# Loads of batch 2's u rows bound behind batch 1's v rows, and two units' row swaps moved from VectorE to DMA

## The chip, the cores and the metric

The kernel runs on one core of a Trainium2 chip. The metric is device time in microseconds (us) of one execution. A core has a matrix engine (TensorE, PE in the profile, with its weight loads as PEld), VectorE (DVE), ScalarE (ACT), GpSimd (POOL) and SyncE (SP), each with an instruction stream of its own that runs in order; they meet at semaphores. SP and POOL issue DMAs, which run on 16 DMA engines.

## The reference

Two layers, one after the other. The first mixes in the frequency domain: a real FFT over the 3008 positions of each of 8 batches (256 channels), a complex 256x256 product with a bias, a soft threshold, and the inverse FFT. The second is a two-layer network over all 24064 rows.

```
def _attn_ref(x, w_r, w_i, b_r, b_i):
    X = np.fft.rfft(x, axis=1)
    Xr, Xi = (X.real.astype(np.float32), X.imag.astype(np.float32))
    Yr = Xr @ w_r - Xi @ w_i + b_r
    Yi = Xr @ w_i + Xi @ w_r + b_i
    lam = 0.01
    Yr = np.sign(Yr) * np.maximum(np.abs(Yr) - lam, 0.0)
    Yi = np.sign(Yi) * np.maximum(np.abs(Yi) - lam, 0.0)
    Y = Yr.astype(np.float64) + 1j * Yi.astype(np.float64)
    return np.fft.irfft(Y, n=x.shape[1], axis=1).astype(np.float32)

def _moe_ref(x, w_in, w_out, s, b):
    h = x @ w_in                      # 256 -> 2048
    r = np.maximum(h, 0.0)
    g = s * (r * r) + b
    return (g @ w_out).astype(np.float32)   # 2048 -> 256
```

## The kernel before

The FFTs are done as matrix products, in two factors each (3008 = 94 x 32 for batches 0 and 1, 64 x 47 for the others). One batch passes through these steps, all with fp16 operands and fp32 in PSUM:

- **u** (`s1_units`, matmul L701 for batch 1, L703 for the others): the first factor of the forward DFT. The copies out of PSUM (`evac`, L248 on ACT or L252 on DVE) go to tiles u, which SP stores to a DRAM buffer ud (L707).
- **us** (`load_us`, L716): four SP loads per batch bring the u rows back in another order, 384 KB each. For batch 1 they follow the last store at once; for the others they are units of the plan (`us_loads`).
- **forward, second factor**: L768 for batch 1 (`fwd_unit` inside `mix_units`), L734 for the others (`fwd_units`), into xt.
- **mix** (`mix_units`): for each of 12 units i, `sum_unit` (L798) and `mix_unit` (L811) do the complex product; DVE adds (L816, which frees the PSUM bank), clips (L821, L822) and subtracts (L823) in slots of a tile called ring. Then four **row swaps** per unit copy 64-row blocks of the result to another slot of ring (lines 827 to 834), either as SP DMAs of 32 KB (L831) or as DVE copies (L833).
- **inverse, first factor** (`inv_unit`, L841): reads the swapped slot four units later; every second unit SP stores v to a DRAM buffer vd (L850, six stores of 256 KB per batch). After the last unit SP loads the v rows back in two loads of 768 KB (L857, tiles vs).
- **inverse, second factor** (`s4_units`, L897): from vs into yt, the rows of the second layer.

The second layer (`first_mm` L952 with the Relu on ACT L959 and the square on ACT L963 or DVE L966; `second_mms` L1010 with the scaling on DVE L1020 and output stores L978, L985 and L993) runs over tiles of 512 (or 480) rows in 16 slots each, the second product one tile behind the first. After a first stage for batch 0 alone, this stream is the backbone: a plan written out by hand (`schedule`) places the units of the other batches' DFTs into its slots. Units of batch 1's `mix_units` lie in slots 24 to 65; batch 2's u loads in slots 75 to 82; `s4_units(1)` begins 11 slots, and `fwd_units(2)` 6 slots, before batch 1's rows begin in the second layer.

The order in which each engine's instructions stand is made by a scheduler when the program is built; `tc.issue_after(ins)` adds an edge, so that what is issued in the block stands behind `ins` on the same engine. Two further things set the order around the change. `evac` and `first_mm` choose between ACT and DVE by a running account of both engines' work (`load`), to which each swap on DVE adds 0.13. And SP's queue is in order: an SP DMA whose data aren't ready, or that must wait for an earlier DMA, holds all behind it.

Of the kernel before, what the change touches and what calls it, by code (L numbers as in the profile page):

```python
# [165 lines left out]
def kernel(  # L166
# [507 lines left out]

    UCH = XCH // 2
    us_loads = {}

    def s1_units(b, more_banks=False):

        old = b == 1  # L680
        rows, n = (96, N2) if old else (P, XH)
        ud = dpool.tile([rows, n, D], F16, name="ud", tag="ud")
        hold = {}
        if old:
            xts[b] = bigpool.tile([P, 2 * DC * CLASSES * L1], F16, name="xt", tag="xt")

        def unit(i):
            c, j = divmod(2 * i, XCH)
            k, ju = divmod(2 * i, UCH)
            if ju == 0:  # L690
                if old and k % 2:
                    w = UCH * D
                    hold["u"] = xts[b][:, k // 2 * w : k // 2 * w + w].rearrange(
                        "p (j d) -> p j d", d=D
                    )
                else:
                    hold["u"] = upool.tile([P, UCH, D], F16, name="u", tag="u")
            ps = any_bank() if more_banks else one_bank()
            rhs = x16[(b, c)][:, j * D : (j + 2) * D]
            if old:  # L700
                nc.tensor.matmul(ps[0:96, :], A_t[0:N1, :], rhs[0:N1], start=True, stop=True)  # L701
            else:
                nc.tensor.matmul(ps, A_2, rhs, start=True, stop=True)  # L703
            u = hold["u"]
            evac(u[0:rows, ju : ju + 2, :], ps[0:rows].rearrange("p (j d) -> p j d", j=2), 512)
            if ju == UCH - 2:
                nc.sync.dma_start(out=ud[:, k * UCH : (k + 1) * UCH, :], in_=u[0:rows])  # L707
            if i == n // 2 - 1 and old:
                for q in range(4):
                    load_us(q)  # L710

        def load_us(q):
            p, g = (P, 6) if old else (2 * SLOTS, GROUPS // 4)
            uv = ud.rearrange("k n d -> (k n) d").rearrange("(q p) d -> p q d", p=p)
            t = uspool.tile([P, g, D], F16, name="us", tag="us")
            nc.sync.dma_start(out=t[0:p], in_=uv[:, g * q : g * q + g, :])  # L716
            us[(b, q)] = t

        us_loads[b] = [lambda q=q: load_us(q) for q in range(4)]
        return [lambda i=i: unit(i) for i in range(n // 2)]  # L720

# [24 lines left out]
    def mix_units(b):  # L746

        old = b == 1
        vd = dpool.tile([NPAIR, P, D], F16, name="vd", tag="vd")
        if not ring:  # L750
            ring.append(bigpool.tile([P, 12, 2, D], F16, name="ring", tag="corr"))
        zt = {}
        hold = {}

        def xf(i):
            w = 3 * DC * P
            i %= 4
            return xts[b][:, w * i : w * i + w].rearrange("p (r c k) -> p r c k", r=3, c=DC)

        def fwd_unit(i):  # L760

            bank = one_bank()
            ps = bank.rearrange("p (r c j k) -> p r c j k", r=2, c=DC, j=2)
            t = us[(b, i // 3)]
            for j in range(2):
                q = (2 * i + j) % 6
                for dc in range(DC):
                    nc.tensor.matmul(  # L768
                        ps[:, :, dc, j, :], t[:, q, dc * P : (dc + 1) * P],
                        F_t[:, 2 * i + j, :], start=True, stop=True,  # L770
                    )
            xt = xf(i)
            evac(xt[:, 1:3].rearrange("p r c k -> p (r c k)"), bank, 512)
            nc.vector.tensor_tensor(out=xt[:, 0], in0=xt[:, 1], in1=xt[:, 2], op=ALU.add)
            load["dve"] += 0.25

        def xs_of(h):
            if old:
                return [xf(2 * h + i)[:, 0] for i in range(2)]
            xt = xts[b]  # L780
            at = slice(2 * P * h, 2 * P * h + 2 * P)
            xs = xspool.tile([P, DC, 2 * P], F16, name="xs", tag="xs")
            nc.vector.tensor_tensor(out=xs, in0=xt[:, 0, :, at], in1=xt[:, 1, :, at], op=ALU.add)
            load["dve"] += 0.38
            return [xs[:, :, i * P : (i + 1) * P] for i in range(2)]

        def x_of(i, r):
            if old:
                return xf(i)[:, 1 + r]
            return xts[b][:, r, :, i * P : (i + 1) * P]  # L790

        def sum_unit(h):

            xs = xs_of(h)
            ps = one_bank().rearrange("p (i e) -> p i e", i=2)
            for i in range(2):
                for dc in range(DC):
                    nc.tensor.matmul(  # L798
                        ps[:, i, :], xs[i][:, dc], W_g[:, dc, 2],
                        start=(dc == 0), stop=(dc == DC - 1),  # L800
                    )
            s = mpool.tile([P, 2, D], F32, name="s", tag="m")
            nc.scalar.copy(out=s, in_=ps)
            load["act"] += 0.6
            hold[h] = s

        def mix_unit(i):
            ps = one_bank().rearrange("p (r e) -> p r e", r=2)
            for r in range(2):
                for dc in range(DC):  # L810
                    nc.tensor.matmul(  # L811
                        ps[:, r, :], x_of(i, 1 - r)[:, dc], W_g[:, dc, r],
                        start=(dc == 0), stop=(dc == DC - 1),
                    )
            t, m = ring[0][:, i % 4], ring[0][:, 4 + i % 2]
            nc.vector.tensor_tensor(  # L816
                out=t, in0=ps, in1=hold[i // 2][:, i % 2].unsqueeze(1).to_broadcast([P, 2, D]),
                op=ALU.add,
            )

            nc.vector.tensor_tensor(out=m, in0=t, in1=low, op=ALU.max)  # L821
            nc.vector.tensor_tensor(out=m, in0=m, in1=high, op=ALU.min)  # L822
            nc.vector.tensor_tensor(out=t, in0=t, in1=m, op=ALU.subtract)  # L823
            load["dve"] += 1.75

            z = ring[0][:, 6 + i % 6]
            for j in range(2):
                for r in range(2):
                    o, a = z[64 * r : 64 * r + 64, j], t[64 * j : 64 * j + 64, r]
                    if i < (H // 2 if old else H - 2):  # L830
                        nc.sync.dma_start(out=o, in_=a)  # L831
                    else:
                        nc.vector.tensor_copy(out=o, in_=a)  # L833
                        load["dve"] += 0.13
            zt[i] = z

        def inv_unit(i):
            ps = one_bank().rearrange("p (j e) -> p j e", j=2)
            z = zt.pop(i)
            for j in range(2):  # L840
                nc.tensor.matmul(  # L841
                    ps[:, j, :], T_t[:, 2 * i + j, :], z[:, j, :], start=True, stop=True
                )
            if i % 2 == 0:
                hold["v"] = vpool.tile([P, 4, D], F16, name="v", tag="v")
            v = hold["v"]
            h = 2 * (i % 2)
            evac(v[:, h : h + 2, :], ps, 512)
            if i % 2 == 1:
                nc.sync.dma_start(  # L850
                    out=vd[2 * i - 2 : 2 * i + 2].rearrange("q p e -> p q e"), in_=v
                )
            if i == H - 1:
                vv = vd.rearrange("q (k n) e -> (q k) n e", n=N2)
                for h in range(2):
                    t = vspool.tile([96, HW, D], F16, name="vs", tag="vs")
                    nc.sync.dma_start(out=t, in_=vv[:, h * HW : (h + 1) * HW, :])  # L857
                    vs[(b, h)] = t

        units = []  # L860

        def put(f, i, n):
            if 0 <= i < n:
                units.append(lambda: f(i))

        for h in range(H // 2 + 2 + old):
            k = h - old
            if not old:
                put(sum_unit, h, H // 2)
            for i in range(2):  # L870
                if old:
                    put(fwd_unit, 2 * h + i, H)
                put(mix_unit, 2 * k + i, H)
                put(inv_unit, 2 * k - 4 + i, H)
            if old:
                put(sum_unit, h, H // 2)
            if k == H // 2 - 1:
                units += [lambda: None] * 2
        return units
# [238 lines left out]
```

## Time and profile before

| what | value |
|---|---|
| median of 3 runs | 846.5 us (846.5 to 850.94) |
| the profiled execution | 849.39 us |
| its span, first to last instruction | 847.6 us |
| mean granted TensorE clock | 0.998 |
| PE busy | 832.4 us (98%) |
| DVE busy | 692.2 us (82%) |
| ACT busy | 647.3 us (76%) |
| DMA queue of SP (q1) | 80.08 MB, 32.9% of 16 engines' span |
| DMA queue of POOL (q0) | 16.00 MB, 11.2% |

"Busy" counts the engine's instructions without those of its sequencer (waits and DMA issues). A wait table names who waited, for whom, and how long in total, how often and at most. A window of the profile gives per engine the busy us and the number of instructions (x), then the granted clock, the DMA engines' share and GB/s. Times inside the execution count from the span's start.

### The profile page before, as it was taken

The numbers are of one execution on the slowest core, as the hardware profiler recorded it, in microseconds if no ns is written. First come the engines' busy times: TensorE is split into PE (matmuls) and PEld (weight loads), VectorE is DVE, ScalarE is ACT, GpSimd is POOL, SyncE is SP. The second block draws the span as 40 slices with busy tenths as digits, with TensorE's granted clock in tenths as the row PEclk, the third lists the DMA queues.
The fourth block names the chain that finished last, engine by engine and source line by source line (L and its number), as shares of the span: only waits on it lengthen the run. The fifth ranks groups of instructions, "written<-read, shape, count | busy, mean of one in ns | idle before, by whom it ended". The sixth has DMA issues, their size and how long they took to land.

```text
span 847.6 us, 17209 instructions
## 1 busy us (share of the span) xinstructions
PE 832.4 (98%) x6726; PEld 597.9 (71%) x6726; DVE 692.2 (82%) x1011; ACT 647.3 (76%) x853; POOL 58.5 (7%) x87
## 2 busy tenths in 40 slices
PE   8999998999999999999999999999999999999998
PEld 6857675767777767766776767766677776766766
DVE  5999995888788888898888888888888878776674
ACT  5988875777887788788887887788777877766663
POOL 4640100000001000000001000000000000000000
PEclk9999999999999999999999999999999999999999
DMA  8965775156543674165722656023640222401111
GB/s 199 184 164 132 200 172 162 37 124 157 154 111 75 157 197 121 59 145 147 188 62 59 166 145 168 32 77 112 162 137 26 61 89 89 113 32 39 38 44 51
DMA packets 109225, 97.18 MB, mean 115 GB/s; under 512 B 10956, under 2 KB 98000, under 8 KB 107800
## 3 DMA queue, kind: packets, MB, share of 16 engines
q1 hardware_dynamic: 102200, 80.08, 32.9%
q0 software_dynamic: 6944, 16.00, 11.2%
q8 instruction: 53, 0.87, 0.4%
q14 instruction: 28, 0.23, 0.1%
HBM read 55.34 MB, written 46.66 MB: 120 GB/s over the span
## 4 chain that ended last, share of the span: by engine, by line
PE 86%; DVE 5%; DMA 3%; ACT 3%; issue 2%; POOL 0%; DVEq 0%; ACTq 0%; SPq 0%; POOLq 0%
PE psa L1010 36%; PE psh L952 35%; PE psf L811 4%; PE psf L897 2%; PE psf L841 2%; PE psf L734 2%; PE psf L798 2%; PE psf L703 2%; ACT rt L959 1%; DVE ring L816 1%; DMA x<-in_x_dram 1%; DVE gt L966 1%; PE psm L528 1%; DMA vd<-v 1%; DMA vs<-vd 1%
## 5 line engine op out<-in xcount | busy, mean ns | idle before, releaser
L959 ACT ACTIVATE rt<-psh 128x1024 f32<-128x1024 f32 (+2 forms) x384 | 387.1, 1009 | 111.3 <-PE psh L952 111.0
L966 DVE TENSOR_TENSOR gt<-rt 128x1024 f16<-128x1024 f32 (+2 forms) x319 | 380.6, 1197 | 103.4 <-ACT rt L959 101.0
L1010 PE MATMUL psa<-w_out_t,gt 128*128 128x256 f16 (+1 forms) x3024 | 455.1, 273 | 0.0
L1010 PEld LDWEIGHTS <-gt 128*128 128x128 f16 (+1 forms) x3024 | 301.3, 101 | 187.2 <-issue 2.0
L952 PE MATMUL psh<-yt,w_in 128*128 128x512 f16 (+1 forms) x1344 | 397.9, 378 | 0.2 <-ACT rt L959 0.2
L952 PEld LDWEIGHTS <-w_in 128*128 128x128 f16 x1536 | 140.8, 98 | 26.2 <-issue 3.5
L1020 DVE SCALAR_TENSOR_TENSOR ost<-psa,s_bc,bias_bc 128x512 f32<-128x512 f32 (+2 forms) x97 | 71.0, 732 | 14.3 <-PE psa L1010 13.3
L963 ACT ACTIVATE gt<-rt 128x1024 f16<-128x1024 f32 (+2 forms) x65 | 68.1, 1048 | 1.7
L248 ACT CAST v<-psf 128x512 f16<-128x512 f32 x83 | 48.1, 580 | 18.4 <-PE psf L841 17.1
L816 DVE TENSOR_TENSOR ring<-psf,s 128x512 f16<-128x512 f32 x84 | 57.4, 683 | 3.9 <-PE psf L811 2.3
L248 ACT CAST yt<-psf 128x480 f16<-128x480 f32 (+2 forms) x72 | 44.1, 623 | 17.2 <-PE psf L897 16.6
L952 PE MATMUL psh<-tail,w_in 128*128 128x512 f16 (+1 forms) x192 | 52.1, 353 | 0.0
L248 ACT CAST u<-psf 128x512 f16<-128x512 f32 (+1 forms) x71 | 41.7, 587 | 11.9 <-PE psf L703 11.8
L811 PE MATMUL psf<-W_g,xt 128*128 128x256 f16 x336 | 50.4, 273 | 0.0
L248 ACT CAST xt<-psf 128x480 f16<-128x480 f32 (+3 forms) x71 | 42.5, 599 | 9.0 <-PE psf L734 8.0
L916 POOL COPY tail<-yt 128x896 f16<-128x896 f16 x6 | 10.0, 1666 | 420.2 <-ACT yt L248 327.1
L821 DVE TENSOR_TENSOR ring<-ring,low 128x512 f16<-128x512 f16 x84 | 35.5, 422 | 2.2
L822 DVE TENSOR_TENSOR ring<-ring,high 128x512 f16<-128x512 f16 x84 | 35.4, 422 | 2.2
L823 DVE TENSOR_TENSOR ring<-ring 128x512 f16<-128x512 f16 x84 | 35.4, 422 | 1.8
L811 PEld LDWEIGHTS <-xt 128*128 128x128 f16 x336 | 32.9, 98 | 3.9
L897 PEld LDWEIGHTS <-vs 96*128 96x128 f16 x448 | 30.2, 98 | 6.5 <-DMA vs<-vd 3.8
L302 POOL DMA_DIRECT2D x<-in_x_dram x36 | 18.7, 528 | 222.9 <-PE psf L703 222.9
(114 smaller groups left out, 541.4 us busy)
## 6 DMA issues: line engine op xcount, KB each, us to landing
out_dram<-ost SPq DMA_DIRECT2D x170, 128.0 KB
us<-ud SPq DMA_DIRECT2D x28, 384.0 KB
vd<-v SPq DMA_DIRECT2D x42, 256.0 KB
vs<-vd SPq DMA_DIRECT2D x14, 768.0 KB
x<-in_x_dram POOLq DMA_DIRECT2D x36, 256.0 KB, 5.1
ud<-u SPq DMA_DIRECT2D x36, 256.0 KB
ring<-ring SPq DMA_DIRECT2D x264, 32.0 KB
out_dram<-ost SPq DMA_DIRECT2D x16, 120.0 KB
```

The costliest lines, as they stand in the source:

```text
L248: return None, nc.scalar.copy(out=dst, in_=src)
L811: nc.tensor.matmul(ps[:, r, :], x_of(i, 1 - r)[:, dc], W_g[:, dc, r], start=(dc == 0), stop=(dc == DC - 1),)
L816: nc.vector.tensor_tensor(out=t, in0=ps, in1=hold[i // 2][:, i % 2].unsqueeze(1).to_broadcast([P, 2, D]), op=ALU.add,)
L821: nc.vector.tensor_tensor(out=m, in0=t, in1=low, op=ALU.max)
L822: nc.vector.tensor_tensor(out=m, in0=m, in1=high, op=ALU.min)
L897: nc.tensor.matmul(ps[:, j * 96 : (j + 1) * 96], vs[(b, h)][:, k, ec * P : (ec + 1) * P], C_t if b == 1 else C_2, start=True, stop=True,)
L952: nc.tensor.matmul(o, w_in_t[dc][:, mc * P : (mc + 1) * P], r, start=(dc == 0), stop=(dc == DC - 1),)
L959: nc.scalar.activation(out=rt[:, :, 0:w], in_=ps[:, :, 0:w], func=AF.Relu)
L963: nc.scalar.activation(out=gt[:, :, 0:w], in_=rt[:, :, 0:w], func=AF.Square)
L966: nc.vector.tensor_tensor(out=gt[:, :, 0:w], in0=rt[:, :, 0:w], in1=rt[:, :, 0:w], op=ALU.mult)
L1010: nc.tensor.matmul(ps[0:size, h, :], gts[(ti, mc // 2)][:, mc % 2, sub * size : (sub + 1) * size], w_out_t[:, mc, :], start=(mc == 0), sto ...
L1020: nc.vector.scalar_tensor_tensor(out=ost[0:size, 0:k], in0=ps[0:size, 0:k], scalar=s_bc[0:size], in1=bias_bc[0:size].unsqueeze(1).to_broad ...
```

## The change

Three edits that belong to two changes. The u loads of batch 2 (L716) are issued inside `issue_after` of the last of batch 1's two v loads (L857), so they stand behind both on SP; before, nothing ordered them but the scheduler. And of batch 1's twelve units, units 6 and 7 make their row swaps as SP DMAs, as units 0 to 5 do, so that DVE copies those of units 8 to 11 alone; the running account of DVE's load is smaller by 8 x 0.13 from there on.

```
     us_loads = {}
+    last_vs = [None]
...
             t = uspool.tile([P, g, D], F16, name="us", tag="us")
-            nc.sync.dma_start(out=t[0:p], in_=uv[:, g * q : g * q + g, :])
+            if b == 2:
+                with tc.issue_after(last_vs[0].ins):
+                    nc.sync.dma_start(out=t[0:p], in_=uv[:, g * q : g * q + g, :])
+            else:
+                nc.sync.dma_start(out=t[0:p], in_=uv[:, g * q : g * q + g, :])
...
                     o, a = z[64 * r : 64 * r + 64, j], t[64 * j : 64 * j + 64, r]
-                    if i < (H // 2 if old else H - 2):
+                    if i < (H - 4 if old else H - 2):
                         nc.sync.dma_start(out=o, in_=a)
                     else:
                         nc.vector.tensor_copy(out=o, in_=a)
...
                     t = vspool.tile([96, HW, D], F16, name="vs", tag="vs")
-                    nc.sync.dma_start(out=t, in_=vv[:, h * HW : (h + 1) * HW, :])
+                    last_vs[0] = nc.sync.dma_start(out=t, in_=vv[:, h * HW : (h + 1) * HW, :])
```

Here H is 12 and `old` is true for batch 1.

## The prediction

> **What bounds the kernel now.** I read the page first: TensorE (PE) is busy 98% of the span and PEclk reads 9 in every slice, so only PE's rare gaps can be won back. The table of what PE waited for names the gaps; its first row is the largest, a later one is DVE's:
>
> ```profile
> PE psf L897 <- DMA vs<-vd: 3.5, 1, 3.5
> ...
> PE psf L703 <- DVE ring L816: 2.1, 4, 0.8
> ```
>
> The first is one wait: the first matmul of the last DFT of batch 1 waits for the first v rows. The stretches around it, busy time by engine, then granted clock, DMA share and GB/s:
>
> ```profile
> 134.16:137.66 3.50, 0.01 (x2) 0.01 (x1) 0.98 (x1) 0.00 (x0) 0.00 (x0) 1.00 1.03 262
> 137.66:139.10 1.44, 1.44 (x17) 1.12 (x18) 0.00 (x0) 1.02 (x2) 0.00 (x0) 1.00 0.99 252
> 139.10:142.50 3.40, 3.40 (x19) 2.02 (x17) 1.16 (x1) 2.04 (x4) 0.00 (x0) 0.50 0.28 94
> ```
>
> PE does nothing for 3.50 us while the DMA engines are full, and 1.44 us after it resumes the clock is at 0.50 for 3.40 us; half of that, 1.70 us, is lost. The event costs 3.49 + 1.70 = 5.19 us.
>
> The chain of waits from 125 us says why the rows are late:
>
> ```profile
> 124.34 0.96 ACT rt L959
> 125.30 6.53 DMA vd<-v
> 131.84 0.02 SPq L857
> 131.86 0.03 issue
> 131.89 5.72 DMA vs<-vd
> ```
>
> The last store of v is issued at 125.30 and lands 6.53 us later; only then SP may issue the v loads, and the first takes 5.72 us. The same store's data were ready long before: the last inverse matmul (L841) starts at 116.41 and ACT's copy of it ends at 117.41. SP's own timeline shows what stood in front:
>
> ```profile
> 116.51 0.34 SPq L716 DMA_DIRECT2D us<-ud  x1
> 116.95 0.49 SPq L850 DMA_DIRECT2D vd<-v  x1
> 117.49 1.33 SPq L716 DMA_DIRECT2D us<-ud  x2
> 118.91 1.13 SPq L850 DMA_DIRECT2D vd<-v  x1
> 120.14 5.11 SPq L978 DMA_DIRECT2D out_dram<-ost  x2
> 125.30 1.21 SPq L850 DMA_DIRECT2D vd<-v  x1
> 126.63 1.13 SPq L716 DMA_DIRECT2D us<-ud  x1
> 131.89 0.82 SPq L857 DMA_DIRECT2D vs<-vd  x2
> ```
>
> Three u loads (384 KB each) fill the queue; the two output stores behind them, elsewhere 0.55 to 0.65 us to issue, hold SP for 5.11. But batch 2's u rows are first used by PE at 144.8 (L734), after the v rows. SP also stood 6.2 us in front of the first u load, waiting for a store of u (SP's waits: L716 on ud), with the fourth v store behind it.
>
> **The u loads.** Read from the built program, SP's order after the last store of u is now: v stores 4 and 5, two output stores, v store 6, both v loads, two output stores, three u loads, two output stores, the fourth u load. POOL's order is the same, and on PE a few units move past two or four neighbouring matmuls. (All times here are those of the trace; what the swaps below win moves both ends of each comparison alike.)
>
> When do the v rows land? The output stores before v store 6 need DVE's L1020, which ends at 117.95; two issues of 0.6 us put v store 6 at 119.2. Its time to land is not in the trace without u loads ahead. By the semaphore records of the trace v store 4, behind one u load, took 3.77 us, v store 6 took 6.53 and v store 5, behind three u loads and the 768 KB table load of POOL (landing 8.9 us), took 10.4. I take 6.53: two output stores and that table load remain ahead. The v loads are then issued at 125.8 (123.0 to 129.6) and the first lands 5.72 us later (5.6 to 6.1 in every other batch), at 131.5 (128.7 to 135.3). PE wants it at 134.16. So the wait goes, with 2.7 us to spare, and only the worst row leaves 1.1 us. The second v load, 8.09 us from issue in this trace, lands near 134.3; its first use is the seventh of fourteen units, some 7 us after the first. Gain: 3.49 us of wait.
>
> With the wait goes the low clock. The row: 3.49 us idle was followed by 3.40 us at half speed; gaps of 0.80 and 0.49 us near 101 and 104 were followed by none. Gain 1.70 us. The Trainium skill, page "TensorE: Matmul & The Clock Gate", section "Why this matters for your kernels", asks for no PE-idle gaps above about 3 us; by it a left-over of 1.1 us would cost 1.1 and not more, which this trace can't show.
>
> What is late next? The u rows. Behind the v loads and two output stores (0.6 us each) the first u load is issued at about 127.9. Its latency: 3.54 us (first u load, free queue) to 10.6 (third, in the jam), so it lands at 131.4 to 138.5; I take 8, between the jam's rows and the free one because 1.5 MB of v loads is ahead: 135.9. PE's first L734 moves up to 144.84 - 5.19 = 139.65. The second u load is needed two units later, the third six; the fourth waits for the second v load and output stores, issued near 134.5 and landing by 145, needed ten units in, past 150. Each is covered, the first by 3.8 us, at worst by 1.1. Nobody else waits on SP there: output stores move by less than 2 us and their buffers (three) are not in PE's list of waits.
>
> **The row swaps of units 6 and 7.** VectorE loses eight copies, 221 ns each by the group of L833, 0.92 us for each unit's four by the timeline:
>
> ```profile
> 92.98 0.92 DVE L833 COPY ring<-ring 64x256 f16<-64x256 f16 x4
> ...
> 97.94 0.92 DVE L833 COPY ring<-ring 64x256 f16<-64x256 f16 x4
> 98.89 1.23 DVE L966 TENSOR_TENSOR gt<-rt 128x1024 f16<-128x1024 f32 x1
> 100.03 0.68 DVE L816 TENSOR_TENSOR ring<-psf,s 128x512 f16<-128x512 f32 x1
> ```
>
> That is 1.85 us off DVE just ahead of the L816 at 100.03 and the one at 103.29, for which PE's L703 stood 0.80 and 0.49 us (a PSUM bank). The built order adds two things. The planner exchanges two squares between ACT and DVE, so the 1.23 us square at 98.89 falls behind the first L816 and another stands ahead of the second. The first L816 thus comes 1.85 + 1.23 us earlier and its gap of 0.80 closes; the second comes 1.85 - 1.22 = 0.63 us earlier while PE comes 0.80 earlier, which makes its gap 0.66. And on PE a pair of L952 (0.43 us) now goes ahead of that second L703, which leaves 0.23. Gain 0.80 + 0.49 - 0.23 = 1.06 us; the ends are 0 (PE waits for another of DVE's results instead) and 1.29.
>
> SP gets eight swaps of 0.60 us each, 4.8 us. Unit 6's go in before v store 2 (94.86 us before), unit 7's between two output stores (96.11). SP stands idle 102.8 to 104.4 and 104.8 to 108.1, so it has caught up by the third v store. Their users: the inverse of unit 6 at 107.94, of unit 7 at 110.33 on PE. Swaps issued behind stores took up to 6.2 us to land (the one at 90.06); unit 7's, issued 98.4 to 100.9, land by 107.1, against 110.33 - 1.06 = 109.3 wanted. Cover 2.2 us; cost nothing, at worst about 1 us. The Trainium skill, page "DMA: Bandwidth & Descriptors", section "Rules for kernel authors", speaks against this step: transfers under 64 KB are mostly overhead, and these are 32 KB where 0.22 us of DVE did the work. [...]
>
> **What moves by itself.** The planner now leans a little more to DVE: over the whole program the squares on ACT go from 62 to 63 and the copies out of PSUM shift by a few either way; DVE is 82% and ACT 76% busy, so their sums decide nothing. But ACT and DVE caught up during the stall. From 134.16 to 150.00 (15.84 us) ACT worked 8.90 us; without the lost 5.19 that is 8.90 in 10.65, 84%, and one square of about 1 us comes to ACT there. I charge 0.5 us (0 to 1.5: one square and a copy). In the later batches the order of u loads and swaps changes by single places; the v loads of batch 2 land at 238.75 against 241.58 wanted, 2.8 us of cover. Zero, within 1 us either way, since PE's gaps from 150 to 830 are 1.3 us in all.
>
> **Sum.** 3.49 + 1.70 + 1.06 - 0.5 = 5.75 us, on the profiled execution's 849.39 us (span 847.6 and 1.8 around it): 843.6. The runs' median is 846.5 with one run at 850.94, so the profiled one lies between; taking the same 5.75 off the median gives 840.75, forecast **840.8 us**.
>
> **Rivals.** First, only part comes off the median: either the two runs at 846.5 already had a shorter wait than the profiled one (the 2.9 us between them is of the size of the clock loss plus a microsecond), or v store 6 takes the 10.4 us of the jam because POOL's table load, not the u loads, held it. Then about 5.75 - 2.9 = 2.85 us, or with 1.1 us of wait left and the clock loss kept 5.75 - 2.8 = 2.95: 843.6. For it: one profile is all there is of the wait; against: SP's blockage, 6 us, is undone whatever the table load does.
>
> Second, slower: PE stops at L734 for u rows instead. It decides once the loss there eats 5.75 us: about 4.05 idle with 1.70 of low clock, so u rows at 143.7, 15.8 us after issue; no u load took over 10.6. Were they to take 21.2 (twice the jam), PE would stand until 149.1, 9.45 us, and lose 11.15 with the clock: 851.9 us. DMA moving 262 GB/s at full share at that place is for it; that the total to be moved is the same is against it.
>
> Third, that the change does nothing: the scheduler could ignore the binding; the built order excludes it.
>
> **Chances.** Forecast 0.66, partial 0.23, slower 0.11. About 0.5% (4.2 us) is what a measurement of this kernel can tell from no change: faster means under 842.3, so the partial case counts as the same. The range: low 838, if both DVE gaps go and nothing is charged (6.5 off: 840.0) and the later gaps (1.3 us) and the launch give 2 us more; high 846, the partial case with its spread. Below and above lie about 2 in 10.
>
> **What would show it.** Right: no PE wait at L897 on the v loads and no half clock near 135 to 145; v store 6 issued near 119, v loads near 126; the gaps at L703 near 101 to 104 shorter; no PE wait of L841 on a swap. Wrong: a PE wait at L734 on u loads, a wait at L897 of over 1 us, or PE gaps that grow after 150.

## The result

| | before | changed |
|---|---|---|
| median of 8 executions each | 846.91 us (846.13 to 851.48) | 843.58 us (842.48 to 845.01) |
| ratio of changed to before | | 0.994, 95% interval 0.9921 to 0.9958 |
| the profiled execution | 849.39 us, span 847.6 | 842.48 us, span 840.7 |

The kernel is 0.6% faster; the forecast was 840.8 us with a range of 838 to 846, so the result lies inside the range, 2.8 us above the forecast. The profiled executions differ by 6.9 us, the medians by 3.3. That difference is explained by the first experiment.

### The profile page after: what moved, and what is told of

Its sections match the earlier page's. It is cut to its first block, busy times and chain, and to the rows that moved or that the text cites. A ratio compares the mean times of both kernels' runs of the same rounds, so it can differ in the third digit from the quotient of the medians.

```text
span 840.7 us, 17217 instructions
## 1 busy us (share of the span) xinstructions
PE 830.2 (99%) x6726; PEld 597.2 (71%) x6726; DVE 692.3 (82%) x1005; ACT 646.5 (77%) x851; POOL 58.3 (7%) x87
## 3 DMA queue, kind: packets, MB, share of 16 engines
q0 software_dynamic: 6944, 16.00, 11.4%
## 4 chain that ended last, share of the span: by engine, by line
PE 89%; DVE 3%; ACT 2%; DMA 2%; issue 2%; SPq 1%; POOL 0%; DVEq 0%; ACTq 0%; POOLq 0%
PE psa L1015 37%; PE psh L957 36%; PE psf L816 4%; PE psf L902 2%; PE psf L803 2%; PE psf L846 2%; PE psf L739 2%; PE psf L704 2%; DMA x<-in_x_dram 1%; ACT rt L964 1%; PE psm L528 1%; DVE ring L821 1%; DVE gt L971 1%; DMA ud<-u 1%; POOL x L289 0%
## 5 line engine op out<-in xcount | busy, mean ns | idle before, releaser
L1015 PE MATMUL psa<-w_out_t,gt 128*128 128x256 f16 (+1 forms) x3024 | 454.3, 273 | 0.0
L1015 PEld LDWEIGHTS <-gt 128*128 128x128 f16 (+1 forms) x3024 | 300.8, 101 | 186.2 <-issue 1.4
L957 PE MATMUL psh<-yt,w_in 128*128 128x512 f16 (+1 forms) x1344 | 397.3, 378 | 0.2 <-ACT rt L964 0.2
L957 PEld LDWEIGHTS <-w_in 128*128 128x128 f16 x1536 | 140.8, 98 | 24.7 <-issue 1.7
L1025 DVE SCALAR_TENSOR_TENSOR ost<-psa,s_bc,bias_bc 128x512 f32<-128x512 f32 (+2 forms) x97 | 71.1, 733 | 12.6 <-PE psa L1015 11.6
L821 DVE TENSOR_TENSOR ring<-psf,s 128x512 f16<-128x512 f32 x84 | 57.4, 684 | 3.7 <-PE psf L816 2.7
L957 PE MATMUL psh<-tail,w_in 128*128 128x512 f16 (+1 forms) x192 | 52.1, 353 | 0.0
L248 ACT CAST u<-psf 128x512 f16<-128x512 f32 (+1 forms) x71 | 41.6, 586 | 12.6 <-PE psf L704 12.5
L816 PE MATMUL psf<-W_g,xt 128*128 128x256 f16 x336 | 50.4, 272 | 0.0
L248 ACT CAST xt<-psf 128x480 f16<-128x480 f32 (+3 forms) x68 | 40.6, 598 | 10.3 <-PE psf L739 9.1
L816 PEld LDWEIGHTS <-xt 128*128 128x128 f16 x336 | 32.9, 98 | 4.0
L846 PE MATMUL psf<-ring,T_t 128*128 128x256 f16 x168 | 32.2, 273 | 0.5 <-DMA ring<-ring 0.2
```

Of the source, the lines that this page charges most:

```text
L248: return None, nc.scalar.copy(out=dst, in_=src)
L816: nc.tensor.matmul(ps[:, r, :], x_of(i, 1 - r)[:, dc], W_g[:, dc, r], start=(dc == 0), stop=(dc == DC - 1),)
L821: nc.vector.tensor_tensor(out=t, in0=ps, in1=hold[i // 2][:, i % 2].unsqueeze(1).to_broadcast([P, 2, D]), op=ALU.add,)
L846: nc.tensor.matmul(ps[:, j, :], T_t[:, 2 * i + j, :], z[:, j, :], start=True, stop=True)
L957: nc.tensor.matmul(o, w_in_t[dc][:, mc * P : (mc + 1) * P], r, start=(dc == 0), stop=(dc == DC - 1),)
L1015: nc.tensor.matmul(ps[0:size, h, :], gts[(ti, mc // 2)][:, mc % 2, sub * size : (sub + 1) * size], w_out_t[:, mc, :], start=(mc == 0), sto ...
```

## The profile after

What PE waited for, in the stretch of 100 to 150 us of the changed kernel (columns: engine and line, whom it waited for, us in total, times, longest). The changed kernel's line numbers are one higher up to the u loads and five higher after them: L704 is the L703 of before, L821 its L816:

```profile
PE psf L704 <- DVE ring L821: 0.6, 1, 0.6
```

It is the only row. The wait for the v rows (3.5 us) has no row any more, and the two waits for DVE near 101 and 104 have become one of 0.57 us at 103.64. The stretches in which the stall and the half clock lay are full, at full clock, with the DMA engines as busy as before at first:

```profile
133.00:136.00 3.00, 3.00 (x34) 2.26 (x32) 1.99 (x2) 2.28 (x4) 0.00 (x0) 1.00 1.09 264
136.00:146.00 10.00, 9.94 (x111) 7.47 (x110) 7.92 (x11) 8.08 (x12) 0.00 (x0) 1.00 0.46 127
```

SP's timeline shows where the v rows got ahead:

```profile
114.69 0.37 SPq L855 DMA_DIRECT2D vd<-v  x1
116.47 1.32 SPq L983 DMA_DIRECT2D out_dram<-ost  x2
117.89 0.51 SPq L855 DMA_DIRECT2D vd<-v  x1
124.71 0.80 SPq L862 DMA_DIRECT2D vs<-vd  x2
125.61 1.25 SPq L983 DMA_DIRECT2D out_dram<-ost  x2
126.90 3.95 SPq L719 DMA_DIRECT2D us<-ud  x2
```

The last v store is issued at 117.89 (125.30 before), the v loads at 124.71 (131.89), and the two output stores ahead of the last v store take 1.32 us to issue where they took 5.11. The blockage has moved to the u loads: two of them now take 3.95 us. By the semaphore records the first v load lands at 130.81, wanted at 133.3; the first u load at 136.98, wanted at 138.80.

On DVE the swaps of units 6 and 7 are gone, and the addition that stood at 100.03 is at 97.62, where it now waits for PE:

```profile
97.62 0.69 DVE L821 TENSOR_TENSOR ring<-psf,s 128x512 f16<-128x512 f32 x1 [0.39 <-PE psf L816]
...
101.75 0.92 DVE L838 COPY ring<-ring 64x256 f16<-64x256 f16 x4
...
102.91 0.68 DVE L821 TENSOR_TENSOR ring<-psf,s 128x512 f16<-128x512 f32 x1
```

The next addition, at 102.91, still stands behind unit 8's four copies. On PE a pair of L957 (the L952 of before) now goes ahead of the matmul that needs it:

```profile
102.48 0.59 PE L957 MATMUL psh<-yt,w_in 128*128 128x512 f16 x2
103.64 0.38 PE L704 MATMUL psf<-x,A 128*128 128x512 f16 x1 [0.57 <-DVE ring L821]
```

Comparing the start of the same matmuls (L1010 and L1015, in order) in the two traces dates the gain: 0.6 us by 112, 6.0 by 143, 6.7 by 178, and 6.7 at the end (between 311 and 596 it is 6.2).

## The experiments

**The kernel before, again.** No edit.

> The kernel before, unchanged, to see how its own executions differ. Theory (the wait for the v rows differs from run to run, since it is what is left when two long DMA queues race): the executions near 846.5 have a span some 3 us shorter than the profiled one of before (847.6), about 844.5, and a mean clock of 1.000 or nearly, since their wait is too short for the half clock; those near 850 have a span of 847 or more and a clock of 0.998. Rival (the wait is the same in all, the start or the launch differs): clock 0.998 and the same wait in all of them, and time minus span varies by 3 us or more.

Twelve executions have a median of 847.96 us, ratio 0.9988 (0.9972 to 1.0004) to 23 more beside them. The profiled one took 845.78 us, span 844.0, and its wait for the v rows was less than half as long:

```profile
PE psf L897 <- DMA vs<-vd: 1.5, 1, 1.5
```

```profile
134.39:135.87 1.48, 0.00 (x1) 0.00 (x1) 0.98 (x1) 0.00 (x0) 0.00 (x0) 1.00 1.06 260
135.87:140.00 4.13, 4.13 (x43) 3.11 (x44) 1.90 (x3) 3.47 (x6) 0.00 (x0) 1.00 0.52 149
```

1.48 us of idle and no half clock after it. So the loss at this place is 1.5 us in one execution and 5.2 in another: the wait is what is left of two long DMA queues, and the queue's time varies. Time minus span varied by 1.0 us over the twelve (1.78 to 2.76), not by 3 or more: the rival falls. The theory's mark of the clock holds only roughly. Over 63 executions of before in the three comparisons the median span is 845.4 us at a mean clock of 0.999 or above (17 of them) and 847.8 at 0.996 or below (29), but the traces show a window of half clock near the start in some executions too (this one has it at 7.6 to 11 us), so a clock of 0.998 doesn't by itself mean the wait. All 63 have a median of 848.68 us against 843.56 for 14 executions of the changed kernel: 5.1 us, though not all on one chip; side by side on one (the last comparison below) it is 848.36 against 843.48, 4.9 us. The 8 executions of before in the result's table were on the short side.

**The binding alone** (units 6 and 7 keep their copies on DVE):

```
-                    if i < (H - 4 if old else H - 2):
+                    if i < (H // 2 if old else H - 2):
```

> The u loads of batch 2 behind the v loads, and six units' swaps left on VectorE. Theory: the wait of the last DFT for the v rows (3.49 us) and the half clock after it are gone, the gaps at L703 near 101 and 104 stay at about 1.3 us in all; span 842 (840.7 + 1.0 to 1.3), median about 1 us above the changed kernel's 843.6. Rival (the swaps are what brings v rows early): a wait of over 1 us for the v rows stays.

Median 844.47 us, ratio 0.9949 (0.9934 to 0.9964), span 842.0. PE's list between 90 and 150 us has one row:

```profile
PE psf L704 <- DVE ring L821: 1.3, 2, 0.8
```

No wait for v rows, no half clock, both gaps for DVE as before. The last v store is issued at 119.41. The theory's numbers hold; the swaps have no part in the v rows.

**The swaps alone** (the kernel before with the other edit):

```
-                    if i < (H // 2 if old else H - 2):
+                    if i < (H - 4 if old else H - 2):
```

> Units 6 and 7 swap by DMA, the u loads of batch 2 not bound. Theory: the gaps at L703 near 101 and 104 shrink from 1.29 to about 0.6 us and the wait for the v rows stays at 3 to 4.5 us with the half clock (PE reaches it a little earlier, the DMA queue has 256 KB more); span 846 to 848, the median within 1.5 us of before. Rival (SP's 4.8 us of extra issues delay everything behind): wait for the v rows over 5 us, median 2 us or more above before.

Median 847.28 us, ratio 0.9979 (0.9964 to 0.9993), span 846.3:

```profile
PE psf L897 <- DMA vs<-vd: 2.8, 1, 2.8
PE psf L703 <- DVE ring L816: 0.6, 1, 0.6
```

The gaps for DVE shrink by 0.72 us (1.29 to 0.57), the wait for v stays and is followed by 3.41 us of half clock. Both as the theory said, the wait a little under its lower bound of 3 us. A wait not expected: 1.0 us at L841 near 310 for a swap of batch 3. One of 0.2 to 1.3 us stands there in all six profiles of kernels with eight units' swaps by DMA, and in none with six, nine or ten. Why an edit in batch 1 does this to batch 3 was not tried; the planner's account, which the edit changes, moves single places of the order there.

**The table load out of the way.** POOL's 768 KB load waits for the first v rows; all else as before:

```
+            nc.gpsimd.tensor_copy(out=T_t[0:1, 0, 0:1], in_=vs[(1, 0)][0:1, 0, 0:1])
             nc.gpsimd.dma_start(out=T_t, in_=T_v_d)
```

> The kernel before, with POOL's 768 KB load of the second inverse table held until the first v rows have landed (a one-element copy on POOL makes it wait), so that it is out of the jam of 117 to 131 us; the u loads stay ahead of the v loads. Theory A (u loads on SP's in-order queue are the cause): SP still issues the fourth u load and the last v store behind the blocked output stores, and the wait stays at 2.5 us or more. Theory B (plain bytes: 768 KB at 262 GB/s are 2.9 us): the wait falls to about 0.6 us and the half clock goes, span 843.0. Theory C (the table load is the cause): the wait goes altogether.

Median 844.52 us, ratio 0.9949 (0.9933 to 0.9964), span 842.7; the wait is 0.2 us without half clock. Its SP:

```profile
119.90 2.87 SPq L979 DMA_DIRECT2D out_dram<-ost  x2
122.82 1.07 SPq L851 DMA_DIRECT2D vd<-v  x1
...
128.87 1.19 SPq L858 DMA_DIRECT2D vs<-vd  x2
```

Theory A falls: with the u loads still ahead the wait is nearly gone. The 0.2 us lie between B's 0.6 and C's none, the span near B's 843.0; one profile of a wait that varies can't part these two. The u loads are not the one cause: of u loads and table load in the DMA queues, taking either away is enough (844.47 and 844.52 us).

**Half of the binding.** Only the last two u loads are bound:

```
-            if b == 2:
+            if b == 2 and q >= 2:
```

> The changed kernel with the first two u loads of batch 2 left free (they stand before the fourth and fifth v store), the last two bound behind the v loads: 768 KB instead of 1536 KB ahead of v. Theory (bytes in front decide: at 262 GB/s each 384 KB u load is 1.5 us; taking out the 768 KB table load brought the wait from 1.5 to 3.5 us down to 0.2): the wait for the v rows is 0 to 0.5 us, no half clock, median equal to the changed kernel's within 1 us. Rival (SP held in order by the blocked stores, whatever the bytes): the wait stays over 1 us, median 845 or more.

The theory of bytes missed, and the rival's numbers came. The wait was 1.9 us (no half clock after it), the median 845.31, ratio 0.9969 (0.9953 to 0.9985). SP shows why:

```profile
117.70 0.34 SPq L721 DMA_DIRECT2D us<-ud  x1
118.14 0.48 SPq L855 DMA_DIRECT2D vd<-v  x1
...
119.84 2.60 SPq L855 DMA_DIRECT2D vd<-v  x1
122.53 1.69 SPq L983 DMA_DIRECT2D out_dram<-ost  x2
124.33 0.56 SPq L855 DMA_DIRECT2D vd<-v  x1
```

The first u load still stands until the last store of u has landed, and the fourth and fifth v stores stand behind it to 118 and 119.8; they were issued at 110.78 and 114.69 in the changed kernel. These two, the two u loads and POOL's table load then queue up within some 3 us, and the last v store goes out at 124.33, between the 123.86 and the 125.30 of the two profiles of before. So order counts as well as bytes. The two come together, for the most part, in one number, the time of the last v store's issue:

| kernel | last v store issued | first v load landed | between | PE's wait |
|---|---|---|---|---|
| changed | 117.89 | 130.81 | 12.9 | none |
| binding alone | 119.41 | 130.76 | 11.4 | none |
| table late | 122.82 | 134.41 | 11.6 | 0.2 |
| before, again | 123.86 | 135.83 | 12.0 | 1.5 |
| swaps alone | 124.13 | 136.40 | 12.3 | 2.8 |
| half bound | 124.33 | 135.40 | 11.1 | 1.9 |
| before | 125.30 | 137.61 | 12.3 | 3.5 |

From issue to v rows it is 11.1 to 12.9 us in these seven profiles, jam or not, and 11.9 to 12.6 in four of the six others below. The other two show that it isn't fixed: 9.8 us with both cures, where the table load is out of the way too, and 14.9 in one profile of nine units (why was not tried). What the change moved is the issue, by 6.0 to 7.4 us.

**The u loads later still.** To try the second rival, they are bound behind four more output stores:

```
-                with tc.issue_after(last_vs[0].ins):
+                with tc.issue_after(last_vs[0].ins), tc.issue_after(last_st[0].ins):
```

(`last_st[0]` is the last output store issued by `store`, and the u loads are units of slots 88 and 89.)

> The changed kernel with the u loads of batch 2 pushed further back on SP, behind six output stores after the v loads (the last of them wait for VectorE's result near 137 us). It puts the second rival of the prediction to the test. Theory: the first u load is issued near 137.6 and lands near 141.5, PE wants it at 139; so PE stands 2 to 4 us at L734 and, if that is over about 2.8 us, gets the half clock as well: median 2 to 5.5 us above the changed kernel's 843.6. Other theory (PE's units can be moved over without loss): no wait at L734 over 0.5 us, median within 1 us.

Median 851.11 us, ratio 1.0034 (1.002 to 1.0049), 7.5 above the changed kernel:

```profile
PE psf L740 <- DMA us<-ud: 4.7, 1, 4.7
```

```profile
141.80:146.50 4.70, 0.03 (x1) 0.00 (x0) 0.95 (x1) 0.00 (x0) 0.00 (x0) 0.99 0.95 216
146.50:150.00 3.50, 3.49 (x28) 2.64 (x29) 1.50 (x3) 1.76 (x3) 0.00 (x0) 0.52 0.53 114
```

The first u load is issued at 139.09 and lands at 146.47. The wait is of the kind the theory named, 0.7 us longer than its upper bound because SP's output stores ran 1.5 us later and the load took 7.4 us, not 3.9. 4.7 idle and 1.7 of half clock are 6.4; a swap of batch 3 adds 1.3. So the median too lies above its upper bound of 5.5.

**More swaps by DMA.** Nine units, then ten, in place of eight:

```
-                    if i < (H - 4 if old else H - 2):
+                    if i < (H - 3 if old else H - 2):      # nine
+                    if i < (H - 2):                        # ten
```

> The changed kernel with unit 8's swaps by DMA too (nine by DMA, three by VectorE). Theory: the gap of 0.57 us at L703 near 104 goes, since unit 8's four copies stand on VectorE ahead of the L816 that it waits for; no new wait; span 840.1, median 0.5 us under the changed kernel's. Rival (another of VectorE's instructions is late there): the gap stays within 0.2 us of 0.57.

> The changed kernel with the swaps of units 8 and 9 by DMA too (ten units by DMA, two by VectorE). Theory (VectorE's copies ahead of L816 cause the gap): the last gap of 0.57 us at L703 near 104 goes; but the swaps of units 8 and 9 are issued from 102 to 108 and their inverse matmuls follow 9 us later, with v store 5 behind, so either cover holds and the span is 0.4 to 0.6 us shorter, or PE waits up to 1.5 us at L841 for a swap. Rival (SP full): the last v store is issued over 2 us later than 117.9 and a wait for the v rows returns.

Nine: median 843.19 us, ratio 0.9942 (0.9925 to 0.9958); the gap near 104 is gone, as the theory said; against it, a wait of 0.3 us for DVE's xt at L739 is new, and the span is 841.4, not 840.1. Ten: median 847.10, ratio 0.9989 (0.9971 to 1.0007). PE waits for a swap, and the clock is halved for 6.83 us:

```profile
PE psf L846 <- DMA ring<-ring: 3.2, 1, 3.2
```

```profile
115.78:118.94 3.16, 0.00 (x1) 0.01 (x1) 1.84 (x4) 0.01 (x1) 0.00 (x0) 0.86 0.68 208
118.94:124.90 5.96, 5.94 (x22) 3.32 (x23) 1.88 (x2) 2.78 (x5) 0.57 (x1) 0.50 0.38 114
```

The wait is twice the upper bound expected. Unit 9's swaps are issued at 111.10 to 113.05 and land by 119.30, behind a store of v that was issued at 109.89 and landed at 118.47. The last v store goes out at 124.65, 6.8 us later than in the changed kernel, the sign that the rival named; PE had lost about as much by then, and no wait for the v rows came back. This execution was a long one (851.82 us), so the size is not typical; the place of the wait is shown.

**Nine units beside the changed kernel, and both cures together.** On one chip; the last is the changed kernel with the late table load above.

> The changed kernel, unchanged, beside the next two on the same chip. Theory: no wait for the v rows in its profiled execution, the gap near 104 again 0.5 to 0.6 us, span 840.7 to 842.0 in most executions, median 843.6 within 0.7 us.

> Nine units' swaps by DMA once more, to compare it with the changed kernel on one chip. Theory: the gap of 0.57 us near 104 is the only thing that it takes away, so its median is 0.3 to 0.7 us under the changed kernel's, which is near what the spread of the executions (1.5 us) lets one see. Rival: it is not faster.

> The changed kernel with the 768 KB table load also held until the first v rows have landed. Theory (once the last v store is issued when its data are ready, nothing is left to win there): the last v store is issued at 118 as in the changed kernel, the v rows land 1 to 3 us earlier, there is no wait either way, median within 0.7 us of the changed kernel's. Rival (the table load collides with the u loads, now behind the v loads): PE waits at L734 and the median is over 1 us higher.

| kernel | median us | ratio to before | 95% interval |
|---|---|---|---|
| changed | 843.48 | 0.9943 | 0.9922 to 0.9965 |
| nine units by DMA | 842.69 | 0.9928 | 0.991 to 0.9946 |
| changed, table late | 843.69 | 0.9939 | 0.9921 to 0.9957 |

The changed kernel repeats. Nine units is 0.8 us under it here (and its other median, 843.19, 0.4 under the result's 843.58, which was not taken beside it), in the direction of the gap of 0.57 us that it closes and of batch 3's wait that it lacks; the intervals overlap, so it is the best version measured, not one shown to be faster. Its cover is used up: one of its two profiles has a first wait for the u rows, and there the v rows land at 132.57, 0.1 us before PE's first use of them at 132.67:

```profile
PE psf L739 <- DMA us<-ud: 0.4, 1, 0.4
```

With both cures the v rows land at 127.71, 3.1 us earlier than in the changed kernel, and that wins nothing.

## Why the prediction was right, and where its sizes were off

- **The wait for the v rows, 3.49 us.** It goes, and by the mechanism named: the binding alone removes it. The last v store was forecast at 119.2, the loads at 125.8, the landing at 131.5; they came at 117.89, 124.71 and 130.81, and in the binding alone, where DVE is not ahead, at 119.41, 125.13 and 130.76. That the u loads alone were to blame was argued, not shown; the late table load cures it too. The first rival's doubt about that table load was half right: in the kernel before, it was as much a cause as the u loads; with them bound it makes the v rows later (130.81 against 127.71) but costs no wait.
- **The half clock, 1.70 us.** It goes with the wait where there was one. But the term was taken from one execution: in another the same kernel waits 1.48 us and has no half clock. The first rival, that only part comes off the median, named exactly this and had a chance of 0.23; the table's medians (3.3 us apart) met its 843.6, and by the prediction's own line of 842.3 this is the partial case. Its other branch, 1.1 us of wait left with the clock loss kept, the runs speak against: after 1.48 and 1.90 us there was none. The larger sample of before (848.68) gives 5.1, near the 5.75 of the sum. The step at fault is taking the profiled execution's gain off a median of three executions, two of which were 2.9 us under the profiled one; off the profiled execution's own 849.39 the same sum gave 843.6.
- **DVE's gaps, 1.06 us.** Mis-sized: 0.72, in the swaps alone and in the changed kernel. The working left 0.66 after the squares and then credited 0.43 for the pair of L952 that moves ahead of the second L703, which made 0.23. The pair did move, but the gap is 0.57. The working let DVE's first addition come 3.08 us earlier; at 97.62 it had to wait 0.39 us for PE and came 2.41 earlier. The second, with two squares between them, came at 102.91, 0.38 earlier and not 0.63. That is 0.25 of the 0.34 us missed, and the wait for PE is its likely reason; PE's coming about 0.1 us earlier than worked out is the rest.
- **The lost catch-up, 0.5 us charged.** Not seen. From 134 to 145 us PE has 10.98 us of work in 11.00 (one window of the changed kernel), with ACT at 9.12. Instead 0.47 us at 178, a gap of before, went as well. That the charge of 0.5 and the over-credit of 0.34 for DVE all but cancelled is luck.
- **The u rows, late next.** The first landed at 136.98 (forecast 135.9), wanted at 138.80: cover 1.8 us, not 3.8. Its load took 10.1 us, the row of the jam, not 8; it was issued 1.0 us earlier than forecast, and PE was there 0.85 us earlier. The second rival did not happen here, but its mechanism exists, and its price was about right: with the u rows late by force, 6.4 us go at that place, where the prediction had put the break-even at 5.75, and the kernel is slower than before (851.11 against 848.68).
- **The swaps, at no cost.** Unit 7's landed by 106.69, forecast 107.1, with no wait in batch 1. Their price shows where the text did not look: near 305, at batch 3's swaps, PE waits 0.2 and 0.5 us in the two profiles of the changed kernel, which the prediction's zero for the later batches did not name.
- **The Trainium skill's rule against small transfers** ("DMA: Bandwidth & Descriptors", "Rules for kernel authors") holds as a cost that must be hidden: the eight 32 KB swaps of units 6 and 7 and the four of unit 8 made PE wait nowhere in batch 1; with the four of unit 9 as well it stood 3.2 us. Each of the eight took 2.3 to 6.7 us from issue to landing, side by side, where DVE's copy takes 0.22.

## What to carry to other kernels

A load that is needed late should not be issued early into a queue through which a store and a reload needed sooner have to pass: read, from the wait backwards, when the last store's data were ready and when it was issued, and the difference (8 us here) is the most by which an order can move it; what that wins is the wait, here 1.5 to 3.5 us, and the half clock where one follows. After the order is right, ask how much cover the moved load has left, since one place further turned the gain into a loss (u loads behind four more stores) or undid it (ten units' swaps by DMA in place of nine). And where one profile's wait is the difference of two long queues, take several executions before its length is put into a sum.

## What the runs showed of the hardware that was not expected

- The half clock after idle time of PE: 1.48 and 1.90 us idle were followed by none, 2.82, 3.49 and 4.68 us by 3.41 us at half speed, and 3.16 us by 6.83, of which the first 0.89 us lay within the wait itself (the clock fell at 118.05, 2.27 us into it). The Trainium skill ("TensorE: Matmul & The Clock Gate", "Why this matters for your kernels") advises against gaps above about 3 us; here 2.82 us was enough.
- From the issue of a 256 KB store to the landing of the 768 KB load that waits for it took 11.1 to 12.9 us in eleven of thirteen profiles, in the jam and out of it, 9.8 in one and 14.9 in another. The jam showed more in the time until SP could issue (two output stores: 1.3 us in the changed kernel, 3.7 and 5.1 in the two profiles of before).
